# Last stage tile by tile in a written order, products of 64 rows, one pass backwards, wo's splits moved and put on GpSimd

## The chip, the cores and the metric

The kernel runs on one core of one Trainium2 chip. The metric is the device time of one execution in microseconds (us); lower is better. Matrix products run on TensorE (PE in the profile; its weight loads are PEld), element-wise work and reductions on VectorE (DVE), activations and copies on ScalarE (ACT), further element-wise work on GpSimd (POOL), and SyncE (SP) issues all DMAs of this kernel.

## What is computed

One block of a network on x, 2048 tokens of 1024 features, all in float32. Cut to what matters:

```python
xn = layernorm(x)
q, k, v = split_heads(xn @ wqkv)                  # 32 heads of 32
pq, pk = q @ w_phi, k @ w_phi                     # one 32x32 matrix for each head
phi_q = concat(softmax(pq), softmax(-pq))         # 64 features a head; phi_k likewise
kv = einsum("bhsf,bhsd->bhfd", phi_k, v)
z = sum(phi_k, over tokens)
o = (phi_q @ kv) / (phi_q @ z + 1e-6)
s = merge_heads(o) @ wo
g = silu((silu(xn @ w1) * (xn @ w3)) @ w2)        # w1, w3: 1024 x 3584; w2: 3584 x 1024
out = x + s * g
```

The quotient of a softmax needs no division of its own: with e = exp(p - max) for the first sign and the like for the second, the kernel keeps e of both signs and rho, the ratio of their two sums for each token and head, and divides once in the last stage.

## The kernel before

A large product is made with one level of a seven-product scheme (`ORDER` names the seven; "A" operands come from the activations, "B" operands from the weights), and each float32 operand is split into a high and a low float32r half (`split`: ACT copies the high half, DVE subtracts it for the low one), so that each product is three passes of matmuls of 128x512.

1. **Start.** The first half of the tokens is normalized and turned, and w_phi is folded into the weights of queries and keys.
2. **Gate and up** (`gate_up`, L595, matmuls on L622). Two halves of tokens, 28 column blocks, seven products each; a step is one product of 12 matmuls. A planner puts side work beside the steps: `at(step, f)` hangs f behind a step, `room` looks for a step with room on DVE. The side work prepares what later stages load: the second half of x, the operands of keys and values, w2's operands (`side_w`, in the second half, with blocks from two rooms of eight that go round), and the split of wo (`side_split`, 16 pieces of 128x512, in the first half; DVE subtracts, and the split is stored to `wo_d`).
3. **Three passes over 8 pairs of token tiles**: the queries (`query_heads`, L882), then two halves of keys and values (`heads`, L817). Each pair needs seven operands of 512 KB, which `reload` fetches a pair ahead. Each pass has seven weight operands of 2 MB: `fetch` loads two of them at the start of the last pair but one of the pass ahead, and five in the last pair, each behind the product that last used its place. The query pass stores e (`e_d`, L871) and rho (L906) to HBM through rooms that the next pass uses for its own features (`room_ev`, L785, filled on L830).
4. **w2** (`product`, L1106). Seven rounds over 8 pairs; `acc` in 16 slabs takes the sums. From the last round on, a slab whose pair is done goes through silu and is stored (`gate`), and is then room for the last stage: e's tiles are loaded (`load_e`) and prepared (`prep`).
5. **Last stage.** For each tile of 128 tokens, `prep` multiplies e by z on POOL (L1082, two instructions of 128x1024), sums on DVE (L1084, two), makes the factors with five short instructions, scales e (L1092, two) and transposes it in blocks of 32 (L1093, two). `attend` multiplies the transposed e by kv with 32-row, 32-column products (L1208) for a batch of two or four tiles and one half of the heads; ACT and DVE split the outcome into `oT`. `finish` makes the product with wo (`project`, L101, 24 matmuls), multiplies by the gate on DVE (L1222, `pm` from PSUM), adds x on POOL (L1223) and stores. For each half of the columns `finish` loads the gate `g` and x `xr`; SP runs in the order that is written, so those loads stand behind the store of the half before:

```python
nc.sync.dma_start(g, g_d[i][:, cs])
nc.sync.dma_start(xr, x[i * P:(i + 1) * P, cs])
```

In this stage only PE and SP run in the written order; on the other engines a scheduler sets it when the kernel is built. The batches are `[[0, 1], [2, 3], [4, 5], [6, 7], [8, 9, 10, 11], [12, 13, 14, 15]]`, and a batch is attended while the last tile of the batch ahead is finished.

## Time and profile before

| | |
|---|---|
| time, median of 3 runs | 2563.17 us (2562.22 to 2564.5) |
| the profiled execution, its own time | 2558.65 us |
| its span, first to last instruction | 2556.7 us |
| busy: PE, DVE, ACT, POOL | 94%, 70%, 34%, 9% of the span |
| mean granted TensorE clock | 0.971 |
| DMA | 586.52 MB, mean 229 GB/s |

A busy PE is not yet a PE at its peak, since its matmuls are pipelined and overlap in the records. So the rows to look for are those in which PE stood idle, with what released it, and those in which the granted clock is under 1.00. The profile speaks of `issue` where an engine waited for nothing that it shows.

### The profile page before, as it was taken

Reading aid. Unit: us, or ns where it says so; the run is one execution under the profiler, and the core shown is the slowest. Engines: PE = TensorE matmul, PEld = TensorE weight load, DVE = VectorE, ACT = ScalarE, POOL = GpSimd, SP = SyncE. Lnnn points to the kernel's source line nnn. Section 1 sums busy time; section 2 is a strip of 40 time slices with the busy share of each in tenths; the row PEclk is TensorE's granted clock in tenths of the full one; section 3 lists DMA queues with packets and bytes.
Section 4 is the critical chain, followed back from the end, with each engine's and each line's share of the span. In section 5 each row is a group of like instructions: output and inputs, shape, how many; then the busy total and the mean of one; then the engine's idle time right before and its main releaser. Section 6 shows DMA issues by size and latency. Waiting matters only on the chain.

```text
span 2556.7 us, 39191 instructions
## 1 busy us (share of the span) xinstructions
PE 2397.5 (94%) x15346; PEld 1965.3 (77%) x15346; DVE 1793.3 (70%) x2827; ACT 856.9 (34%) x1501; POOL 239.8 (9%) x206
## 2 busy tenths in 40 slices
PE   7999999999999999999969999999999999788388
PEld 6888877888888888887848878888888887566266
DVE  8777787755888888746746656657778887945641
ACT  6454555433455545432311111243222223300000
POOL 1000000000000000002310000001111112223321
PEclk9999999999999999999989999999999999988689
DMA  5346899978888887659897587344444336723333
GB/s 216 132 166 217 294 386 376 349 246 253 280 290 285 301 293 265 235 212 347 295 411 286 175 341 244 134 183 173 173 165 151 107 144 205 267 98 126 117 119 118
DMA packets 290793, 586.52 MB, mean 229 GB/s; under 512 B 23856, under 2 KB 141232, under 8 KB 287920
## 3 DMA queue, kind: packets, MB, share of 16 engines
q1 hardware_dynamic: 290608, 584.02, 64.4%
q8 instruction: 121, 1.98, 0.3%
q14 instruction: 64, 0.52, 0.1%
HBM read 378.93 MB, written 205.00 MB: 228 GB/s over the span
## 4 chain that ended last, share of the span: by engine, by line
PE 77%; DMA 9%; DVE 7%; issue 3%; POOL 2%; ACT 1%; SPq 1%; POOLq 0%; DVEq 0%; ACTq 0%
PE bankb L622 22%; PE bankb L1106 11%; PE bankc L622 11%; PE bankb L817 7%; PE banka L622 6%; PE bankc L1106 5%; PE bankc L817 3%; PE banka L1106 3%; PE bankb L882 2%; DMA acc<-e_d 2%; PE banka L817 2%; DMA xr<-in_x 1%; POOL ez L1082 1%; PE pm L101 1%; POOL g L1223 1%
## 5 line engine op out<-in xcount | busy, mean ns | idle before, releaser
L93 DVE TENSOR_TENSOR bo<-rw,bo 128x512 fp32r<-128x512 f32 x336 | 230.9, 689 | 160.2 <-ACT bo L92 158.5
L92 ACT CAST bo<-rw 128x512 fp32r<-128x512 f32 x336 | 206.5, 617 | 27.9 <-PE banka L622 5.8
L1106 PE MATMUL bankb<-bo,as 128*128 128x512 f32 x816 | 201.5, 389 | 3.5 <-DVE acc L1118 3.5
L1106 PEld LDWEIGHTS bankb<-bo,as 128*128 128x128 f32 x816 | 153.0, 188 | 36.1 <-DVE acc L1118 4.4
L622 PE MATMUL bankb<-op0S,bo 128*128 128x512 f32 x672 | 163.6, 392 | 5.0 <-ACT u L656 3.1
L622 PE MATMUL bankb<-op0A,bo 128*128 128x512 f32 x672 | 160.4, 393 | 5.1 <-DVE u L664 4.2
L622 PE MATMUL bankc<-op0S,bo 128*128 128x512 f32 x672 | 162.5, 391 | 0.3 <-DVE op0S L93 0.3
L622 PE MATMUL bankb<-op1S,bo 128*128 128x512 f32 x672 | 161.4, 389 | 0.0
L622 PE MATMUL bankc<-op1S,bo 128*128 128x512 f32 x672 | 161.2, 389 | 0.0
L622 PE MATMUL bankb<-op1A,bo 128*128 128x512 f32 x672 | 157.6, 390 | 0.0
L101 PE MATMUL pm<-wos,oT 128*128 128x512 f32 x576 | 154.2, 428 | 2.9 <-DVE g L1222 2.9
L1106 PE MATMUL bankc<-bo,as 128*128 128x512 f32 x576 | 148.3, 391 | 4.7 <-DVE as L93 4.7
L622 PEld LDWEIGHTS bankb<-op0A,bo 128*128 128x128 f32 x672 | 124.8, 188 | 33.2 <-DVE u L664 6.5
L622 PEld LDWEIGHTS bankb<-op0S,bo 128*128 128x128 f32 x672 | 124.9, 188 | 32.9 <-ACT u L656 4.3
L622 PEld LDWEIGHTS bankb<-op1A,bo 128*128 128x128 f32 x672 | 125.9, 188 | 27.4 <-DVE u L664 1.3
L622 PEld LDWEIGHTS bankb<-op1S,bo 128*128 128x128 f32 x672 | 126.0, 188 | 26.5 <-ACT u L656 0.3
L622 PEld LDWEIGHTS bankc<-op1S,bo 128*128 128x128 f32 x672 | 126.1, 188 | 26.2
L622 PEld LDWEIGHTS bankc<-op0S,bo 128*128 128x128 f32 x672 | 125.3, 188 | 26.3 <-DVE op0S L93 0.7
L101 PEld LDWEIGHTS pm<-wos,oT 128*128 128x128 f32 x576 | 119.0, 209 | 31.6 <-DVE g L1222 3.3
L862 POOL TENSOR_TENSOR eq<-q,mm 128x512 f32<-128x512 f32 x24 | 25.3, 1053 | 1220.9 <-DVE mm L860 1163.4
L1106 PEld LDWEIGHTS bankc<-bo,as 128*128 128x128 f32 x576 | 108.2, 188 | 28.9 <-DVE as L93 6.4
L1208 PE MATMUL po<-acc,kvr 32*32 32x64 f32 (+1 forms) x3072 | 46.6, 283 | 80.4 <-issue 35.0
(245 smaller groups left out, 4502.1 us busy)
## 6 DMA issues: line engine op xcount, KB each, us to landing
rw<-in_w SPq DMA_DIRECT2D x112, 512.0 KB, 5.1
hr<-h_d SPq DMA_DIRECT2D x56, 512.0 KB, 3.4
h_d<-h SPq DMA_DIRECT2D x111, 256.0 KB, 5.4
xoS<-xo_d0S SPq DMA_DIRECT2D x48, 512.0 KB, 7.9
xoS<-xo_d1S SPq DMA_DIRECT2D x48, 512.0 KB, 3.8
xoA<-xo_d0A SPq DMA_DIRECT2D x36, 512.0 KB, 7.8
xoA<-xo_d1A SPq DMA_DIRECT2D x36, 512.0 KB, 3.5
e_d<-eq SPq DMA_DIRECT2D x32, 512.0 KB, 7.6
```

The costliest lines, as they stand in the source:

```text
L92: nc.scalar.copy(hi, src)
L93: (by or nc.vector).tensor_sub(lo, src, hi.bitcast(F))
L101: nc.tensor.matmul(p, xT[dch][:, a], w(dch, b), start=n == 0, stop=n == 3 * ND - 1)
L622: nc.tensor.matmul(bank[b], bos[tb, f][bn][:, w, k], ao[an][:, u, k], start=first and n == 0, stop=LAST[b] == an and n == 11, skip_group_c ...
L817: nc.tensor.matmul(bank[b], xo[an][:, u, k], wb[bn][:, w, k], start=an in ("A11", "A12", "S1") and n == 0, stop=LAST[b] == an and n == 11, ...
L862: eng.tensor_sub(e[:, :, 0], p3, mm[:, 0, :].unsqueeze(2).to_broadcast([P, 16, DH]))
L882: nc.tensor.matmul(bank[b], xo[an][:, u, k], wb[bn][:, w, k], start=an in ("A11", "A12", "S1") and n == 0, stop=LAST[b] == an and n == 11, ...
L1082: nc.gpsimd.tensor_mul(ez[c], e_slab(t, c), zb[c])
L1106: nc.tensor.matmul(bank[b], t[:, u, pos + k], bos[kb, bn, k][:, w], start=first and n == 0, stop=LAST[b] == an and n == 5, skip_group_chec ...
L1208: nc.tensor.matmul(ev[32 * j:32 * j + 32, a, k], kvr[c][sl, j, s, k], et[sl, :, 4 * k + j, s], start=s == 0, stop=s == 1, skip_group_check ...
L1223: (nc.vector if i + 1 == NT else nc.gpsimd).tensor_add(g, g, xr)
```

## The change

- **Last stage.** All five engines run in the written order, one tile t to a step. A step makes the first half of wo's product for t, the pair sums of t+2, the small products of t+1 for one half of the heads, twelve matmuls of the second half of t, the small products for the other half of the heads, and twelve more.
- **64 rows.** e is stored with the sign outside the head (`p (s h f)`), and loaded so that a partition block of 64 holds both signs of 32 tokens. `attend` then multiplies 64 rows by 32 columns, and sums over the signs inside the product: 32 matmuls for a tile and half of the heads, where it had been 128 for two or four tiles. The denominator's sum over the signs is a product with a 0/1 matrix (`add_pairs`, a matmul of 128x64), and the factors become a reciprocal and two products with `w_all`, which holds 1 and rho.
- **Loads ahead of stores.** g and x are loaded a tile ahead and whole (512 KB each), ahead of the stores of the tile.
- **Second pass backwards.** The first pass of keys and values goes from pair 7 to pair 0, so that at both changes of pass the operands in place are used again, and a `reload` of 3.5 MB falls away. The first two weight operands of the next pass are fetched in the fourth and fifth pair, not both in the seventh.
- **wo's splits** go from the first to the second half of gate and up, every ninth step, and their subtraction from DVE to POOL. `side_w` uses three groups of five blocks.

```diff
-    def side_split(d, src, s0):
-        r = []
 
         def load():
-            r.append(flat(blk("wso")))
-            nc.sync.dma_start(r[0], src)
+            nc.sync.dma_start(blk2(15), src)
+
+        def do():
+            t = qp.tile([P, 2, 512], R, name="wso", tag="q")
+            split(t[:, 0], t[:, 1], blk2(15), nc.gpsimd)
+            at(s0 + 6, lambda: nc.sync.dma_start(d, t.bitcast(F)))
 
         at(s0, load)
-        store_quad(s0 + 4, d, lambda: r[0], "wso")
+        at(s0 + 4, do)
...
-        side_split(wo_d[c][k], wo[k * P:(k + 1) * P, c * 512:(c + 1) * 512], FIRST_STEP + 64 + 11 * m // 2)
+        side_split(wo_d[c][k], wo[k * P:(k + 1) * P, c * 512:(c + 1) * 512], HALF + 10 + 9 * m)
...
-        for i in range(len(pairs)):
-            nxt, end = {}, i + 1 == len(pairs)
+        order = range(len(pairs))[::-1] if c == 1 else range(len(pairs))
+        for pos, i in enumerate(order):
+            nxt, end = {}, pos + 1 == len(pairs)
...
-                        if i + 2 == len(pairs) and not last:
-                            for m in range(2):
-                                wbn.update(fetch(3 + c, m))
-                        if not (end and last):
-                            nxt.update(reload((i + 1) % len(pairs)))
+                        if pos in (3, 4) and not last:
+                            wbn.update(fetch(3 + c, pos - 3))
+                        if not end:
+                            nxt.update(reload(order[pos + 1]))
...
-            xo = nxt
+            xo = xo if end else nxt
...
             elif i == 4:
-                prep(0)
+                factors(0)
+                z_sums(1)
+                scale(0, 0)
+            elif i == 5:
+                add_pairs(1, "kv")
+                scale(0, 1)
                 load_e(2)
             elif i == 6:
-                prep(1)
+                factors(1)
+                scale(1, 0)
                 load_e(3)
+            elif i == 7:
+                z_products(2)
...
-    in_order(ENG.SP, ENG.PE)
+    in_order(ENG.SP, ENG.PE, ENG.DVE, ENG.Pool, ENG.Activation)
...
+            for j in range(4):
+                for a in range(2):
+                    sl = slice(64 * a, 64 * a + 64)
+                    nc.tensor.matmul(po[32 * j:32 * j + 32, a, 64 * k:64 * k + 64], kvs[sl, j, c, k], et[sl, :, 4 * k + j],
+                                     start=True, stop=True, skip_group_check=True)
...
+    for t in range(NT):
+        load_e(t + 4)
+        p = out_half(t, 0)
+        if prev:
+            gated(t - 1, 1, prev, False)
+            store_out(t - 1, 1)
+        load_g(t + 1)
+        z_sums(t + 2)
+        z_products(t + 3)
+        scale(t + 1, 1)
+        gated(t, 0, p, t + 1 == NT)
+        store_out(t, 0)
+        add_pairs(t + 2, "us")
+        lows = [attend(t + 1, 0)]
+        factors(t + 2)
+        scale(t + 2, 0)
+        prev = out_half(t, 1, lambda: lows.append(attend(t + 1, 1)))
+        for do in lows:
+            if do:
+                do()
```

Here `out_half` is wo's product for one half of the columns (24 matmuls, with `mid` called after twelve), `gated` the product with the gate and the sum with x, `z_products` the two products on POOL, `z_sums` the two sums on DVE and a product with `w_all`, `factors` the reciprocal and a product, `scale` one scaling and one transpose.

How the order changes is shown at three places. On PE at the start of the last stage, before; `po` is the outcome of the small products, `pm` that of wo's, and a row's last number counts matmuls:

```order
L1106 MATMUL bankb<-bo,as 128x512 x6
L1208 MATMUL po<-acc,kvr 32x64 x256
L101 MATMUL pm<-wos,oT 128x512 x33
L101 MATMUL pm<-late,oT 128x512 x12
L101 MATMUL pm<-wos,oT 128x512 x3
L1208 MATMUL po<-acc,kvr 32x64 x128
L101 MATMUL pm<-wos,oT 128x512 x24
```

The same place in the changed kernel, where `us` is the outcome of the pair sums:

```order
L1133 MATMUL bankb<-bo,as 128x512 x6
L1252 MATMUL po<-acc,kvs 32x64 x64
L1267 MATMUL pm<-wos,oT 128x512 x24
L1105 MATMUL us<-own 128x64
L1252 MATMUL po<-acc,kvs 32x64 x32
L1267 MATMUL pm<-wos,oT 128x512 x6
L1267 MATMUL pm<-late,oT 128x512 x6
L1252 MATMUL po<-acc,kvs 32x64 x32
```

The 256 small products that stood ahead of the first product with wo are 64, and the bursts of 128 between the tiles are two of 32 for each tile.

On DVE in the middle of the last stage, before, one tile's rows:

```order
L1084 TENSOR_REDUCE own<-ez 128x32 x2
L1222 TENSOR_TENSOR g<-pm,g 128x512
L1086 TENSOR_TENSOR own<-own 128x32
L1087 TENSOR_TENSOR own<-own 128x32
L1088 RECIPROCAL own<-own 128x32
L1089 TENSOR_TENSOR own<-own 128x32
L1092 TENSOR_TENSOR acc<-acc,own 128x1024 x2
L1093 STREAM_TRANSPOSE acc<-acc 128x1024 x2
L93 TENSOR_TENSOR oT<-po,oT 128x4x4x32 x2
```

The same engine in the changed kernel, one step:

```order
L1275 TENSOR_TENSOR g<-pm,g 128x512
L1098 TENSOR_REDUCE own<-ez 128x32 x2
L1099 TENSOR_TENSOR own<-own,rho 128x64
L1119 TENSOR_TENSOR acc<-acc,own 128x1024
L1120 STREAM_TRANSPOSE acc<-acc 128x1024
L1275 TENSOR_TENSOR g<-pm,g 128x512
L1111 RECIPROCAL own<-us 128x64
L1112 TENSOR_TENSOR own<-own,rho 128x64
L1119 TENSOR_TENSOR acc<-acc,own 128x1024
L1120 STREAM_TRANSPOSE acc<-acc 128x1024
L1258 TENSOR_TENSOR oT<-po,oT 128x2x4x64 x2
```

The work for one tile, which stood together, is cut into pieces that belong to the tiles t, t+1 and t+2, and the two rows on `oT`, for which PE's next tile waits, stand at the end of the step.

On SP where the query pass goes over into the first pass of keys and values, before; `op3` are the weights of that pass, `xo` the operands of a pair, `e_d` and `rho_d` the stores of the query pass:

```order
L871 DMA e_d_236<-eq 128x1024
L167 DMA op3T_11001<-wkv_d1T_114 128x4096
L871 DMA e_d_232<-eq 128x1024
L871 DMA e_d_236<-eq 128x1024
L906 DMA rho_d_244<-rho 128x64
L587 DMA xoA_11066<-xo_d0A_87 128x1024
L587 DMA xoA_11068<-xo_d0A_88 128x1024
L587 DMA xoS_11070<-xo_d0S_89 128x1024
```

The same place in the changed kernel:

```order
L863 DMA e_d_236<-eq 128x1024
L167 DMA op3T_10964<-wkv_d1T_114 128x4096
L863 DMA e_d_232<-eq 128x1024
L863 DMA e_d_236<-eq 128x1024
L899 DMA rho_d<-rho 128x2x32
L579 DMA xoA_11029<-xo_d1A_94 128x1024
L579 DMA xoA_11031<-xo_d1A_95 128x1024
```

The operands behind the last store are those of the second pair of the new pass (the changed kernel's first pair is pair 7, whose operands are in place); before, seven operands of the first pair had been queued ahead of these stores, and those of the second behind them.

More of the change, by code (lines that the diff above doesn't have):

```diff
@@ L542, in side_w @@
                 at(at_, then)
-        for m in slots:
-            free[m] = at_
+        free[u % 3] = at_
         assert at_ < len(events) - 3 * 7 - 4, at_
-    taken, free = [6], {m: HALF + 14 for m in range(6)}
     def side_store(m, s0):
@@ L805, in tile_kernel, with heads @@
     pkv, out_now = None, []
-    def heads(i, xo, wb, steps, pend):
+    def heads(first, last, xo, wb, steps, pend):
         nonlocal pkv
-        bank, first, last = {}, i == 0, i + 1 == len(pairs)
+        bank = {}
         for b, an, bn in ORDER:
@@ L1032, in tile_kernel @@
         load_b(0, n)
-    wos, zb, kvr, ez = {}, [], [], []
+    wos, xrs, ezs, us = {}, [], [], {}
     def load_wo(k):
@@ new lines, in add_pairs, with factors, scale @@
+    def add_pairs(t, tag):
+        if t >= NT:
+            return
+        us[t] = ps.tile([P, 512], F, name="us", tag=tag, bufs=1)[:, :64]
+        nc.tensor.matmul(us[t], own[:, :P], part_of(t, 0), start=True, stop=True)
+    def factors(t):
+        if t >= NT:
+            return
+        r, by = part_of(t, 1), part_of(t, 2)
+        nc.vector.reciprocal(r, us.pop(t))
+        nc.vector.tensor_mul(*(v.rearrange("p (c g h) -> p c g h", c=2, g=2) for v in (by, r)), w_all[:, t])
+    def scale(t, c):
+        if t >= NT:
+            return
+        e = e_slab(t)[:, c]
+        e3 = e.rearrange("p (n f) -> p n f", f=DH)
+        nc.vector.tensor_mul(e3, e3, part_of(t, 2)[:, 32 * c:32 * c + 32].unsqueeze(2).to_broadcast([P, H, DH]))
+        nc.vector.transpose(et_slab(t, c), e)
@@ L1146, in tile_kernel @@
                 if new is None:
[L1147 removed]
+                    for k in range(2 + 2 * BNAMES.index(bn), 4 + 2 * BNAMES.index(bn)):
                         load_wo(k)
@@ L1159, in tile_kernel @@
             if end:
-                for k in range(3, 9):
+                for k in range(2, 8):
                     load_wo(k)
@@ new lines, in out_half, with gated @@
+    def out_half(t, c, mid=None):
+        p = ps.tile([P, 512], F, name="pm", tag="mm", bufs=3)
+        n = 0
+        for h in range(2):
+            for k in range(4):
+                for a, b in PASSES:
+                    nc.tensor.matmul(p, oTs[t, h][:, a, k], wos[c, 4 * h + k][:, b], start=n == 0, stop=n == 3 * ND - 1)
+                    n += 1
+            if h == 0 and mid:
+                mid()
+        return p
+    def gated(t, c, p, last):
+        cs = slice(c * 512, c * 512 + 512)
+        nc.vector.tensor_mul(gs[t][:, cs], p, gs[t][:, cs])
+        (nc.vector if last else nc.gpsimd).tensor_add(gs[t][:, cs], gs[t][:, cs], xrs[t % 2][:, cs])
```

243 lines of the change are left out of this document (114 added, 129 removed).

## The prediction

> **What bounds the kernel now.** I read the waits of PE over the whole run first, because PE is busy almost everywhere and only its stops can be won back.
>
> ```profile
> PE po L1208 <- issue: 35.0, 15, 4.3
> PE po L1208 <- DVE acc L1093: 31.4, 1, 31.4
> PE bankb L817 <- ACT ev L830: 14.2, 1, 14.2
> PE po L1208 <- DVE oT L93: 13.2, 4, 6.2
> PE bankb L882 <- DMA xoA<-xo_d1A: 4.9, 1, 4.9
> PE bankc L1106 <- DVE as L93: 4.7, 4, 2.5
> PE bankb L622 <- DVE u L664: 4.2, 4, 1.4
> PE bankb L1106 <- DVE acc L1118: 3.7, 3, 2.0
> PE bankc L817 <- DMA op3T<-wkv_d1T: 3.6, 1, 3.6
> PE bankb L1106 <- DVE af L93: 3.4, 2, 2.2
> PE bankb L622 <- ACT u L656: 3.1, 3, 1.2
> PE bankb L1106 <- ACT af L92: 2.5, 1, 2.5
> PE bankb L817 <- DMA op3T<-wkv_d1T: 1.7, 1, 1.7
> ```
>
> Columns are microseconds in total, times, and the longest. Four places stand out. L1208, the small products of the last stage, waited 79.6 us (35.0 + 31.4 + 13.2). L882 and L817, where the query pass goes over into the first pass of keys, waited 24.4 us (14.2 + 4.9 + 3.6 + 1.7). L1106, w2's last round, 14.3 us. L622, gate and up, 7.3 us. I then took the windows that hold these places.
>
> ```profile
> 2139.00:2223.00 84.00, 68.81 (x280) 52.37 (x278) 74.78 (x106) 29.37 (x42) 27.99 (x14) 0.96 0.61 224
> 2223.00:2548.00 325.00, 241.39 (x3841) 194.31 (x3840) 153.93 (x199) 20.05 (x34) 94.77 (x54) 0.84 0.37 127
> 1284.00:1345.00 61.00, 36.62 (x140) 28.95 (x140) 26.30 (x45) 10.71 (x13) 7.54 (x9) 0.82 1.01 409
> 320.00:512.00 192.00, 184.66 (x852) 151.87 (x851) 152.65 (x239) 98.05 (x180) 0.00 (x0) 1.00 1.04 371
> ```
>
> After the length come busy times of PE, PEld, DVE, ACT and POOL, then granted clock, DMA share and GB/s. In the last stage (second row) no engine is full: DVE 154 of 325 us, POOL 95, DMA 37%, and PE 241 with a clock of 0.84. It is a chain of waits, not a full engine, so a better order can win much there. In the other two rows the DMA is full (1.01 and 1.04 of its share), and there only fewer or other transfers help.
>
> **The last stage, PE's side.** The timeline of PE gives the prices.
>
> ```profile
> 2223.99 2.45 PE L1208 MATMUL po<-acc,kvr 32*32 32x64 f32 x231 [0.79 <-DVE acc L1118]
> 2230.71 0.38 PE L1208 MATMUL po<-acc,kvr 32*32 32x64 f32 x25 [4.27 <-issue]
> 2261.49 7.33 PE L101 MATMUL pm<-wos,oT 128*128 128x512 f32 x24
> 2282.37 8.32 PE L101 MATMUL pm<-wos,oT 128*128 128x512 f32 x36
> 2290.53 2.88 PE L101 MATMUL pm<-late,oT 128*128 128x512 f32 x12
> 2476.89 3.02 PE L1208 MATMUL po<-acc,kvr 32*32 32x128 f32 x209
> 1385.50 0.77 PE L802 MATMUL pkv<-ev 128*32 128x34 f32 x64
> 1386.20 3.00 PE L817 MATMUL bankb<-op3T,xoS 128*128 128x512 f32 x12
> 2546.78 0.84 PE L101 MATMUL pm<-wos,oT 128*128 128x512 f32 x3
> 2553.65 0.34 SPq L1224 DMA_DIRECT2D out<-g  x1
> ```
>
> 36 matmuls of wo's product start within 8.16 us (2290.53 - 2282.37), 0.227 us each, so one tile's 48 take 10.9 us. A small product has two records (231 + 25 for the first 128). The new burst is 32 products, 64 records, of 64 columns. It no longer shares the array by sixteen but by eight, so the nearest row is that of 128 columns by sixteen: 3.02 us / 209 = 14.4 ns, 0.92 us for 64. The lower bound is 2.45 / 231 = 10.6 ns, 0.7 us; the upper bound is twice that, 1.4 us. I take 1.05 us, which leaves 0.1 for the change of shape, because 64 records of L802 between large products hold PE for 0.70 us (1386.20 - 1385.50) in all. The pair-sum matmul, which no row shows, I put at 0.3 us: no less than two small records, 0.03, no more than two slots of a large matmul, 0.45, and nearer to these because it stands alone. A step of PE is then 10.9 + 2 x 1.05 + 0.3 = 13.3 us.
>
> The `issue` stops come after 231 records of a burst (second row) and in no burst of 64 of L802. The new bursts have 64, so I let these 35 us go, and keep their return as a rival. The Trainium skill, TensorEngine Tiling (Array Packing), section Key Properties, says that a change of tiling mode drains TensorE. The change has four such changes in a step, against some two for a tile before; L802's row prices the pair at under 0.1 us, so the drain is in the 1.05.
>
> **The last stage, DVE's side.** These are the groups of the same stage (count, busy, mean ns).
>
> ```profile
> L1084 DVE TENSOR_REDUCE own<-ez 128x32 f32<-128x1024 f32 x29 | 35.2, 1215 | 76.2 <-POOL ez L1082 76.2
> L1092 DVE TENSOR_TENSOR acc<-acc,own 128x1024 f32<-128x1024 f32 x30 | 35.8, 1227 | 0.4
> L1093 DVE STREAM_TRANSPOSE acc<-acc 128x1024 f32<-128x1024 f32 x32 | 38.3, 1224 | 0.1
> L1222 DVE TENSOR_TENSOR g<-pm,g 128x512 f32<-128x512 f32 x32 | 22.0, 686 | 60.5 <-DMA xr<-in_x 44.9 <-DMA g<-g_d 8.0 <-PE pm L101 7.6
> L93 DVE TENSOR_TENSOR oT<-po,oT 128x512 fp32r<-128x512 f32 x32 | 21.8, 681 | 35.5 <-ACT oT L92 35.5
> L1088 DVE RECIPROCAL own<-own 128x32 f32<-128x32 f32 x15 | 5.2, 349 | 0.4
> L1082 POOL TENSOR_TENSOR ez<-acc,zb 128x1024 f32<-128x1024 f32 x28 | 66.0, 2377 | 93.5 <-DMA acc<-e_d 91.1 <-DVE own L1084 2.4
> L1223 POOL TENSOR_TENSOR g<-g,xr 128x512 f32<-128x512 f32 x30 | 38.5, 1284 | 150.5 <-DVE g L1222 140.6 <-DMA xr<-in_x 5.6 <-issue 4.3
> 2388.44 9.24 POOL L1082 TENSOR_TENSOR ez<-acc,zb 128x1024 f32<-128x1024 f32 x4 [4.88 <-DMA acc<-e_d]
> 2394.36 1.06 DVE L1086 TENSOR_TENSOR own<-own 128x32 f32<-128x32 f32 x1
> 2395.46 2.26 DVE L1087 TENSOR_TENSOR own<-own 128x32 f32<-128x32 f32 x1
> 2398.14 0.19 DVE L1089 TENSOR_TENSOR own<-own 128x32 f32<-128x32 f32 x1
> ```
>
> A step of DVE holds two gate products, two sums, two scalings, two transposes and two subtractions: 2 x (0.69 + 1.22 + 1.23 + 1.22 + 0.68) = 10.1 us, and a reciprocal and two short products, some 0.35 + 2 x 0.19, together 10.8; since neighbours overlap by under 0.1, about 10.1. POOL has 2 x 2.38 + 2 x 1.28 = 7.3 us. Both are under 13.3, but they are not free of each other. L1086 and L1087 read two operands from SBUF; beside POOL's products they took 1.06 and 2.26 us, ending where a POOL instruction ends (9.24 / 4 = 2.31 us apart), while L1089, clear of POOL, took 0.19. The sums, transposes and the rows that read PSUM show no such stretch.
>
> So I lay one step along time from DVE's first row. Gate product to 0.7; sums to 3.0. POOL adds from 0.7 to 2.0 and begins its first e product there, to 4.4. The short product with `w_all` waits for that, to 4.6 (wait 1.4). POOL's second e product is in line first, to 7.0, and the scaling waits for it (2.3). Scaling and transpose to 9.3, gate product to 9.9; POOL adds to 11.2, and the second short product, after the reciprocal at 10.3, waits for that (0.9). Scaling and transpose to 13.7, two subtractions to 14.9. Without waits it is 10.1, with them 14.9; PE is asked for 13.3. The step is therefore DVE's, 14.9 us, and PE stands about 1.6 us in each, most of it ahead of the subtractions of `oT`.
>
> The Trainium skill, GPSIMD Engine Reference, section Key points, says that GpSimd shares its SBUF interfaces with VectorE and contends with instructions that have two SBUF inputs. The trace agrees (2.26 against 0.19 us). Without the rule the step would be PE's 13.3 us.
>
> Thirteen steps at 14.9 are 193.7 us; two without their pair sums and e products 2 x 13.2; the last tile 10.9: 231.0. Ahead of them I put 7 us: two bursts, the copy and subtraction of `oT`, and the last evictions and silus of w2 that stand ahead on DVE and ACT (0.8 us at least by the 0.79 in the first timeline row; 10 at most). At the end come a product and a sum of 0.69 on DVE, the issue of 0.34 and the landing, from 2553.99 to the span's end, 2556.7: 4.7 us with hand-overs. Together 243 us. Before, the stage ran from the end of w2, 2223.2 (2223.99 - 0.79), to 2556.7, 333.5 us. **Gain 90.5 us**, between 64 (a step of 16.9) and 115 (a step of 13.3 and a start of 4).
>
> Loads: e comes in four parts of 32 partitions, 1 MB in all, g, x and the stores are 1.5 MB: 2.5 MB in 14.9 us is 168 GB/s, while the third window row shows 409. g and x are ordered a step ahead. I cost them at nothing; their cover is a whole step.
>
> **The change of pass.** At the end of the query pass DMA is full. Before, the last two pairs ask for two reloads of 3.5 MB, 14 MB of weights and 4 MB of e, 25 MB in some 38 us. The room of the last e is free only when its store has landed behind all that: the 14.2 us. Now 3.5 + 10 + 4 MB are left. The last pair begins its weights 2.7 us after its start, and 10 + 2 MB at 0.41 MB/us land by 32; the fifth product of the new pass, which adds to a bank that ACT must first copy into that room, is due at about 30 (19 + 4 x 2.72). With the copy and the backlog of the pair before I leave 5 us of 24.4: **gain 19**, between 13 and 24. The two weights put into the fourth and fifth pair make 7.5 MB per 19 us there, just under what DMA gives; I allow nothing for it beyond this range. The other change of pass has no stop in the list.
>
> **w2's last round.** DVE had 74.8 of 84 us. It loses one scaling with its transpose (2.4 us) and three sums that were made early for later tiles (3.7), about 6 us. Of 14.3 us of stops and the slow clock (0.96) I take **7 back**, between 0 and 14.
>
> **wo's splits.** They leave the stretch with a DMA share of 1.04: 16 x (0.25 + 0.5) MB = 12 MB less over some 220 us, 55 of 371 GB/s. I take **6 us** of the 7.3, between 0 and 7. Where they go, PE has no stop, so the stores, the ACT copies and 16 subtractions on POOL (1.28 us each by L1223) find cover; DVE's two-operand rows may wait for each, and the `q` tiles go round faster. **Cost 1.5 us**, between 0 and 8.
>
> The sum is 90.5 + 19 + 7 + 6 - 1.5 = 121 us. The profiled execution took 2558.65, 1.95 more than its span, so it would take 2437.7. The median of the runs is 4.5 higher; from it, 2563.2 - 121 = 2442.
>
> **Rivals.** (a) POOL and DVE fall so that the waits vanish or lie under PE: step 13.3, thirteen steps x 1.6 = 21 us less and a little at the start, 2419. For it: the order is free to drift. Against it: POOL has work ready at each of the three places. (b) The step is longer: `issue` stops return, since a step still asks for 356 instructions of PE in bursts, or the chain from the copy of `oT` binds: step 17, 27 us more, 2469. (c) The change of pass and gate and up keep their stops, as DMA stays full: 25 us lost, 2467.
>
> (d) Slower. PE's clock falls to half for the whole stage. Row 2261.49 shows 24 matmuls in 7.33 instead of 5.44 us after a burst with a stop, and the stage's clock is 0.84. Were it half throughout, a tile's 48 matmuls cost 21.8 us, the bursts about 3 and the pair sums 0.5: a step of 25.3, 10.4 more than forecast, and 15 steps and the last tile are 401 + 12 against 333.5; with the other gains of 30.5 the time is 2612. It turns the sign from 12 slow steps of 16 (121 / 10.4). Against it: L802's bursts between large products run at clock 1.00.
>
> ```profile
> 1408.00:1472.00 64.00, 64.00 (x645) 51.93 (x644) 38.02 (x52) 11.45 (x15) 0.79 (x6) 1.00 0.51 179
> ```
>
> Only bursts of 2 us with a stop of 2 us or more behind them lost it. The Trainium skill, TensorE: Matmul & The Clock Gate, Part 1, asks for an idle window of about 3.4 us; by that rule stops of 1.6 us leave the clock alone. The trace has it falling after a burst and a stop of 4 us together, which fits if a burst of small products counts as idle.
>
> **How the numbers follow.** Forecast 0.57, (a) 0.15, (b) 0.14, (c) 0.06, (d) 0.07; 0.01 for no change, a mild (d) that eats just the gain. Faster is 0.57 + 0.15 + 0.14 + 0.06 = 0.92. A measurement of this kernel can tell about 0.2%, 5 us, from no change. The forecast alone spans 2424 to 2462 by its terms' bounds taken in part; down to (a) with a cheap burst, 2408, and up to (b) and (c) with a bad start, 2482, leave out (d) and tails.
>
> **What would show it.** Right: bursts of 64 records near 1 us without `issue`; steps of 14.9 us with stops of PE before `pm` by `oT`; DVE rows L1099, L1112 and L1119 stretched; under 6 us of stops where pass 0 ends; granted clock near 1.00 in the last stage. Wrong: steps of 13.3 or 17; `issue` or clock 0.5 in the last stage; new waits on L614 in the second half of gate and up; waits of DVE for g or xr.

## The result, and the profile after

The changed kernel takes 2459.05 us (2455.37 to 2463.51), against 2563.84 us for the kernel before beside it: ratio 0.9592, interval 0.9574 to 0.9609. The forecast was 2442. The profiled execution took 2455.37 us with a span of 2453.6; before it was 2558.65 and 2556.7, so the two spans differ by 103.1 us where 121 were forecast.

These are the waits of PE after the change (total, times, longest; L1267 is wo's product, L1252 the small products, L1105 the pair sums, L810 the keys' product, L874 the queries', L1133 w2):

```profile
PE pm L1267 <- DVE oT L1258: 16.1, 12, 7.5
PE bankb L810 <- ACT ev L823: 15.5, 1, 15.5
...
PE bankb L1133 <- ACT af L92: 6.3, 2, 3.9
...
PE us L1105 <- DVE own L1099: 2.2, 1, 2.2
PE pm L1267 <- DMA wos<-wo_d: 1.9, 3, 1.3
PE bankb L874 <- ACT q L880: 1.7, 2, 1.2
```

The 35.0 us of `issue` and the 31.4 us on the transposes are gone. Of the waits that the prediction lists, two are larger than before: the one for ACT's copy `ev` at the change of pass, 15.5 us where it was 14.2, and w2's for ACT's half of the split (`af`), 6.3 where it was 2.5.

Where the stages begin is read from each product's rows: duration, then first and last start. First the kernel before, then the changed one.

```profile
L882 PE MATMUL bankb<-op2B,xoA x96: 389/389/667, 1143.9 to 1293.1; 128*128 128x512 f32 x96
L1106 PE MATMUL bankb<-bo,af x288: 388/389/793, 1667.8 to 2201.1; 128*128 128x512 f32 x144
```

```profile
L874 PE MATMUL bankb<-op2B,xoA x96: 387/389/628, 1141.4 to 1287.4; 128*128 128x512 f32 x96
L1133 PE MATMUL bankb<-bo,af x288: 388/389/796, 1654.7 to 2193.6; 128*128 128x512 f32 x144
```

Differences of first starts are the stages' lengths. The last stage begins at 2223.2 before, as the prediction has it, and at 2206.1 after (its first row below).

| stage | before | after | gain | forecast |
|---|---|---|---|---|
| up to the first query product | 1143.9 | 1141.4 | 2.5 | 6 - 1.5 |
| queries' and keys' passes | 523.9 | 513.3 | 10.6 | 19 |
| w2 | 555.4 | 551.4 | 4.0 | 7 |
| last stage | 333.5 | 247.5 | 86.0 | 90.5 |

One step of the last stage after the change, from the timeline of PE, DVE and POOL:

```profile
2264.51 5.30 PE L1267 MATMUL pm<-wos,oT 128*128 128x512 f32 x22 [0.80 <-DVE oT L1258]
2266.99 4.73 POOL L1090 TENSOR_TENSOR ez<-acc,zb 128x1024 f32<-128x1024 f32 x2
2267.93 1.53 DVE L1099 TENSOR_TENSOR own<-own,rho 128x64 f32<-128x64 f32 x1
2269.39 3.42 DVE L1119 TENSOR_TENSOR acc<-acc,own 128x1024 f32<-128x1024 f32 x1
2269.65 0.33 PE L1105 MATMUL us<-own 128*128 128x64 f32 x2
2269.91 0.86 PE L1252 MATMUL po<-acc,kvs 64*32 64x64 f32 x64
2279.32 5.29 PE L1267 MATMUL pm<-wos,oT 128*128 128x512 f32 x22 [0.81 <-DVE oT L1258]
```

From one large product to the same one a step later is 14.81 us (2279.32 - 2264.51). The first scaling (L1119) takes 3.42 us, where the kernel before had 1.227 on average; POOL's two e products end inside it, at 2271.72 (2266.99 + 4.73), and 1.09 us later it is done. The start of the stage, from the first small products to the second step's first large product, with the queue of SP (`SPq`) in it:

```profile
2206.12 1.71 PE L1252 MATMUL po<-acc,kvs 64*32 64x64 f32 x128
2208.53 6.01 PE L1267 MATMUL pm<-wos,oT 128*128 128x512 f32 x24 [0.70 <-ACT oT L1257]
2214.37 1.56 SPq L1032 DMA_DIRECT2D wos<-wo_d  x2
2216.80 1.62 SPq L1038 DMA_DIRECT2D g_d<-acc  x2
2219.30 0.32 SPq L1238 DMA_DIRECT2D g<-g_d  x1
2229.89 0.69 DVE L1275 TENSOR_TENSOR g<-pm,g 128x512 f32<-128x512 f32 x1 [11.78 <-DMA g<-g_d]
2234.49 7.35 PE L1267 MATMUL pm<-wos,oT 128*128 128x512 f32 x22 [7.50 <-DVE oT L1258]
```

DVE, now in written order, stands 11.78 us at the first gate product, because the load of `g` is ordered behind wo's last loads and the stores of silu. PE stands 7.5 us behind it, and its next 22 matmuls take 7.35 us, not 5.30. Counted, like the step above, from the third matmul of the first large product, which here starts at about 2208.98 (2208.53 + 2 x 0.227), the first step lasts 25.5 us, against 14.81 for a later one.

### The profile page after: what moved, and what is told of

It is laid out like the page before. It is cut to its first block, busy times and chain, and to the rows that moved or that the text cites. A ratio compares the mean times of both kernels' runs of the same rounds, so it can differ in the third digit from the quotient of the medians.

```text
span 2453.6 us, 37229 instructions
## 1 busy us (share of the span) xinstructions
PE 2373.6 (97%) x14354; PEld 1941.4 (79%) x14354; DVE 1837.6 (75%) x2795; ACT 854.8 (35%) x1501; POOL 268.5 (11%) x233
## 4 chain that ended last, share of the span: by engine, by line
PE 77%; DVE 12%; DMA 6%; issue 3%; ACT 1%; POOL 0%; SPq 0%; DVEq 0%; POOLq 0%; ACTq 0%
PE bankb L614 21%; PE bankb L1133 11%; PE bankc L614 10%; PE bankb L810 7%; PE bankc L1133 6%; PE banka L614 5%; PE bankc L810 3%; PE bankb L874 3%; PE banka L1133 3%; DVE acc L1119 2%; PE banka L810 2%; PE bankc L874 1%; PE pm L1267 1%; DVE own L1098 1%; DVE bo L93 1%
## 5 line engine op out<-in xcount | busy, mean ns | idle before, releaser
L1133 PE MATMUL bankb<-bo,as 128*128 128x512 f32 x816 | 200.9, 389 | 0.0
L1133 PEld LDWEIGHTS bankb<-bo,as 128*128 128x128 f32 x816 | 153.2, 188 | 31.8
L1267 PE MATMUL pm<-wos,oT 128*128 128x512 f32 x576 | 145.3, 402 | 18.7 <-DVE oT L1258 16.1
L1133 PE MATMUL bankc<-bo,as 128*128 128x512 f32 x576 | 150.2, 396 | 0.8 <-ACT as L92 0.7
L1267 PEld LDWEIGHTS pm<-wos,oT 128*128 128x128 f32 x576 | 107.1, 191 | 48.8 <-DVE oT L1258 21.8
L1133 PEld LDWEIGHTS bankc<-bo,as 128*128 128x128 f32 x576 | 109.6, 191 | 25.4 <-ACT as L92 2.0
L93 POOL TENSOR_TENSOR wso<-room,wso 128x512 fp32r<-128x512 f32 x16 | 24.2, 1512 | 961.4 <-ACT wso L92 845.0
L1145 DVE TENSOR_TENSOR acc<-bankb,acc 128x512 f32<-128x512 f32 x152 | 104.1, 686 | 27.0 <-PE bankb L1133 19.8
```

The source lines that it names most:

```text
L93: (by or nc.vector).tensor_sub(lo, src, hi.bitcast(F))
L1133: nc.tensor.matmul(bank[b], t[:, u, pos + k], bos[kb, bn, k][:, w], start=first and n == 0, stop=LAST[b] == an and n == 5, skip_group_chec ...
L1145: nc.vector.tensor_add(c, pb, c)
L1267: nc.tensor.matmul(p, oTs[t, h][:, a, k], wos[c, 4 * h + k][:, b], start=n == 0, stop=n == 3 * ND - 1)
```

## Experiments

All times are medians. The interval of a ratio is about 0.0017 to either side, 4 us, so smaller differences are read from the traces. A ratio is against the kernel before, run beside it; between two kernels of the table the interval is wider, some 6 us by an estimate from the two.

| kernel | us | ratio | interval |
|---|---|---|---|
| changed kernel | 2459.05 | 0.9592 | 0.9574 to 0.9609 |
| passes forward | 2468.12 | 0.9618 | 0.9602 to 0.9634 |
| splits back in the first half | 2461.08 | 0.9594 | 0.9580 to 0.9608 |
| splits on DVE | 2454.88 | 0.9570 | 0.9555 to 0.9584 |
| e stored by ACT | 2453.03 | 0.9566 | 0.9549 to 0.9583 |
| no e products | 2440.31 | 0.9519 | 0.9505 to 0.9533 |
| sums later | 2443.88 | 0.9535 | 0.9519 to 0.9550 |
| g early | 2450.41 | 0.9559 | 0.9545 to 0.9574 |
| e stored by ACT, late weights | 2453.51 | 0.9572 | 0.9558 to 0.9586 |
| third room | 2457.92 | 0.9584 | 0.9562 to 0.9606 |
| before, batches of two | 2555.77 | 0.9972 | 0.9960 to 0.9985 |
| five edits | 2419.46 | 0.9439 | 0.9420 to 0.9457 |
| six edits | 2420.36 | 0.9440 | 0.9426 to 0.9453 |

### Does POOL set the step?

**No e products.** From the first step on, POOL's two products of e with z are left out.

```diff
         z_sums(t + 2)
-        z_products(t + 3)
         scale(t + 1, 1)
```

> The changed kernel, but from the first step of the last stage on GpSimd's two products of e with z are left out (so the denominators of tiles 3 to 15 are wrong), and nothing else. Theory (DVE's short products and scalings wait for GpSimd's e products on the shared SBUF interface, and so DVE sets the step of 14.8 us): the stretched rows L1119 go back from 3.4 to 1.23 us and L1099 from 1.5 to 0.2, the step falls to PE's own 13.2 to 13.4 us, PE's stops before pm and po go under 0.3 us a step, and 12 to 13 steps x 1.5 = 18 to 20 us go: 2436 to 2441. Rival (the hand-over from PE to DVE and back over the copy of oT sets the step, GpSimd only fills slack): the rows get shorter but PE still stops for oT by over 0.8 us a step and the gain is under 6 us, 2453 to 2459.

**Sums later.** All the work, in another order: `z_sums` is cut into its sums (`z_reduce`) and its short product (`z_scale`).

```diff
+    z_reduce(2)
+    z_products(3)
...
-        z_sums(t + 2)
-        z_products(t + 3)
+        z_scale(t + 2)
         scale(t + 1, 1)
...
-        scale(t + 2, 0)
+        scale(t + 2, 0, lambda: (z_reduce(t + 3), z_products(t + 4)))
```

The function given to `scale` runs between its product and its transpose.

> The changed kernel with all its work, in another written order on DVE and GpSimd: the sums of the denominators of tile t+3 and GpSimd's e products of t+4 come after the second scaling of the step, ahead of its transpose, so that the e products run beside a transpose, a subtraction and a gate product, none of which reads two operands from SBUF, and the short products and the two scalings find GpSimd idle. Theory (waits of DVE for GpSimd set the step): laid out by hand, the step falls from 14.8 to about PE's 13.2 to 13.6 us, so 12 to 20 us go: 2439 to 2447; DVE's L1119 scaling back at about 1.23 us. Rival (the number of DVE's own operations, 10.1 us, with the hand-overs to PE and ACT in the written order, or GpSimd's own chain, sets the step): under 6 us, 2453 to 2459, or slower since a later sum delays the pair-sum product of PE.

The same 160 us of the last stage of the changed kernel, without e products, and with later sums (busy PE, PEld, DVE, ACT, POOL; clock, DMA share, GB/s):

```profile
2254.00:2414.00 160.00, 145.89 (x1949) 113.66 (x1948) 158.15 (x142) 12.95 (x22) 77.53 (x44) 1.00 0.58 168
```

```profile
2254.00:2414.00 160.00, 160.00 (x2148) 129.55 (x2148) 137.71 (x159) 14.12 (x24) 33.21 (x25) 1.00 0.62 180
```

```profile
2254.00:2414.00 160.00, 159.88 (x2148) 129.16 (x2147) 153.90 (x159) 14.11 (x24) 83.05 (x47) 1.00 0.65 185
```

DVE was the full engine: 158.15 of 160 us, with 142 operations. Without e products it does 159 in 137.71 us, PE is full, and the step, from the same product of PE twice, is 13.12 us (2317.38 - 2304.26). With later sums it is the same, read from two pair sums (2325.77 - 2312.65):

```profile
2312.65 0.33 PE L1116 MATMUL us<-own 128*128 128x64 f32 x2
2325.77 0.33 PE L1116 MATMUL us<-own 128*128 128x64 f32 x2
```

Without e products the time falls by 0.0073 of the kernel before, 19 us (0.9592 - 0.9519). With later sums the 83.05 us of POOL's work are all there, PE is as full, and the time still falls by 0.0057, 15 us. The 4 us between the two are within the intervals; part of them is in the start, where the stop for `oT` is 10.6 us with later sums and 8.2 without e products. Theory shown: DVE's wait for POOL set the step, and the written order placed it there.

### The start of the last stage

**g early.** The first `load_g` is written ahead of wo's last eight loads, in w2's last round.

```diff
                 if new is None:
+                    if an == "S1":
+                        load_g(0)
...
-    load_g(0)
     for c in range(2):
         attend
```

> The changed kernel, but the loads of g and x for the first tile of the last stage are written ahead of the last eight loads of wo in the last round of w2, where they stood behind them and behind stores of g. Theory (the stop of 7.5 us at the start of the last stage is DVE waiting for g, which stands in SP's row): the wait of DVE for g goes, the stop shrinks to 1 to 3 us, and the kernel gains 4 to 7 us: 2452 to 2455. Rival (DMA is full there, so what is taken from g is put on wo's loads or e's): the stop stays over 5 us or moves to PE waiting for wos, gain under 2 us: 2457 to 2460.

```profile
PE pm L1271 <- DVE oT L1262: 8.7, 11, 0.9
```

The stop of 7.5 us has gone: the longest is 0.9. The wait for wo's loads rose by 1.0 us (1.9 to 2.9). By the ratios it gains 0.0033, 8 us, and in the trace the last stage is 7.5 us shorter (from 2206.86 to 2446.8). That is the stop itself; whether the slow matmuls behind it (7.35 - 5.30 = 2.05) came on top can't be told from this, since a stop of 2.4 us for wo's loads, with slow matmuls behind it, took the place of one of 1.3.

### The change of pass

**Passes forward.** All passes go from pair 0 to 7, reload at the change, and fetch two weights in the seventh pair, as before.

```diff
-        order = range(len(pairs))[::-1] if c == 1 else range(len(pairs))
+        order = range(len(pairs))
...
-            xo = xo if end else nxt
+            xo = nxt
```

> The changed kernel with its three passes all forward, both reloads at the changes of pass back, and the first two weights fetched together in the seventh pair, as before. Reading of the trace: the change took the stops at the end of the query pass from 24.4 to about 18 us, so undoing it costs 6 to 8 us, some 2466 us, and the stop on ACT ev is near 14 us again. The forecast's price of the turn was 19 us: if that was right and something else ate it, the time is near 2478 us.

```profile
PE bankb L810 <- ACT ev L823: 13.2, 1, 13.2
PE bankb L874 <- DMA xoA<-xo_d1A: 5.3, 1, 5.3
PE bankc L810 <- DMA op3T<-wkv_d1T: 3.9, 1, 3.9
PE bankb L810 <- DMA op3T<-wkv_d1T: 2.1, 1, 2.1
```

24.5 us of stops, as before the change (24.4); the changed kernel has 17.9 there (15.5 + 1.7, and 0.7 for an operand's reload). Turning back and fetching the two weights earlier are together worth those 6.6 us, and 0.0026 or 7 us by the ratios; no run parts the two. What holds the rest is in the timeline of the changed kernel: the start of the last query pair, SP's queue, the copy, and PE behind it.

```profile
1279.60 12.33 SPq L863 DMA_DIRECT2D e_d<-eq  x4
1284.92 2.88 PE L874 MATMUL bankb<-op2B,xoA 128*128 128x512 f32 x12
1295.14 0.42 SPq L167 DMA_DIRECT2D op3T<-wkv_d1T  x1
1307.65 3.32 SPq L863 DMA_DIRECT2D e_d<-eq  x2
1329.91 0.59 ACT L823 COPY ev<-bankb 128x512 f32<-128x512 f32 x1 [19.28 <-DMA rho_d<-rho]
1330.55 4.82 PE L810 MATMUL bankb<-op3T,xoS 128*128 128x512 f32 x12 [15.55 <-ACT ev L823]
```

SP stands at the stores of the pair ahead, whose e has not been made yet by ACT, so the first weight is ordered at 1295.14, 10.2 us after the pair's start. The copy waits for the pair's third store, issued at 1307.65; the trace's answer on that one store gives its time to landing:

```profile
DMA to landing us min/median/max: 22.2/22.2/22.2
```

That is 1329.85, just ahead of the copy. The releaser that the row names, `rho_d`, was ordered at 1313.28 and took 17.6 us, to 1330.9, so it can't have been what the copy waited for.

**e stored by ACT.**

```diff
-        nc.sync.dma_start(e_d[pairs[i][j]][:, c], ef)
+        nc.scalar.dma_start(e_d[pairs[i][j]][:, c], ef)
...
-                nc.sync.dma_start(rho_d.rearrange(
+                nc.scalar.dma_start(rho_d.rearrange(
```

> The changed kernel with the stores of e and rho in the query pass issued by ACT, not by SP. Theory: the weights of the next pass start late because SP, which works in order, stands at the stores of the pair before, and the last e then lands behind 12 MB; with the stores on another engine's queue the weights start within 3 us of their place and the store no longer stands behind them, so the stop of 15.5 us falls under 4 and the time to about 2446 us. Rival: the volume binds, 14 MB at 0.41 MB/us take 34 us in any order; then the stop stays above 10 us, on the weights if not on ACT ev, and the time is 2455 to 2460 us.

```profile
1288.95 5.76 SPq L167 DMA_DIRECT2D op3T<-wkv_d1T  x3
1325.34 5.49 PE L810 MATMUL bankb<-op3T,xoS 128*128 128x512 f32 x12 [9.22 <-ACT ev L823]
```

The weights start 6 us earlier, 2.9 us after the pair's start (1286.04, seven products of 2.72 us ahead of the pass's end at 1305.08), and the stop falls to 9.2 us. That lies between the two expectations: SP's hold was a part, and the rest needed another cause. The third store now lands 15.9 us after its order, at 1324.68. From the first weight's order to there the DMA is full, and it moved 14.42 MB where the prediction had 10 + 2:

```profile
1288.95:1324.68 35.73, 27.17 (x120) 22.15 (x118) 21.09 (x38) 8.42 (x10) 6.23 (x6) 0.94 1.00 404
DMA packets 2054, 14.42 MB, mean 404 GB/s; under 512 B 466, under 2 KB 466, under 8 KB 1412
```

**Late weights.** On top of that edit, the last two weights two products later.

```diff
-    NEXT = ({0: 2, 1: 3, 2: 4, 3: 5, 4: 6},
+    NEXT = ({0: 2, 1: 3, 2: 4, 5: 5, 6: 6},
```

> The changed kernel with e's and rho's stores issued by ACT (the run before of that kind took 2453.0 and left a stop of 9.2 us on the copy that waits for e's last store) and with the last two of the five weight operands that the last query pair fetches ordered two products (5.4 us) later, so that the third e store of the pair has some 2 to 4 MB less ahead of it. Theory (the store lands late because of the volume ordered ahead of it): the stop of ACT's copy shrinks from 9.2 to 0 to 5 us, nothing waits for the two weights, and 4 to 8 us go: 2445 to 2449. Rival (the weights, not the store, are the true limit, since DMA is full up to the fifth product of the new pass): the stop moves to PE waiting for op3 operands, about the same sum: 2452 to 2456.

It did not test its theory: the stop stayed at 9.5 us, because the orders hardly moved. The fifth weight was ordered 16.67 us after the first with the old table (1305.62 - 1288.95) and 17.20 with the new (1303.70 - 1286.50), rows of `op3T` in SP's timeline. SP's own waits in this stretch name what held them, with the old table and then with the new:

```profile
SPq L167 <- DMA op3T<-wkv_d1T: 10.5, 2, 5.7
SPq L167 <- DMA op3T<-wkv_d1T: 11.0, 2, 5.7
```

The fourth and the fifth order waited until the first and the second weight had landed: the first, ordered at 1288.95, took 10.5 us, to 1299.45, and the fourth went out at 1299.51. So the pace of the landings set these orders, not the table.

**Third room.** The first features and values of the keys go into two `q` tiles.

```diff
     def room_ev():
+        if firsts:
+            e, v = firsts
...
+        if c == 0:
+            firsts += [quad("ev", F), quad("ev", F)]
```

> The changed kernel, but the first features and values of the keys' pass go into two free rooms of the q pool (free because the pass turns back and loads no operands for the next pair) instead of the room of the last query pair's e; nothing else. Theory (the 15.5 us stop at the change of pass is the wait of one ACT copy for the store of e out of that room, which lands late behind 12 MB): the copy no longer waits, the next one that needs the old room comes three products (8 us) later and finds it free or nearly so, the stop of ACT ev goes to 0 to 5 us, and with the slow clock behind it 11 to 17 us go: 2442 to 2448. Rival (DMA volume is the limit itself, whatever waits for it, since 12 MB have to land in some 30 us): PE stops about as long for operands of the new pass (op3 weights) or for the next copy, gain under 6 us, 2453 to 2459.

```profile
PE bankc L817 <- ACT ev L838: 15.0, 1, 15.0
```

The rival held. The stop went to the next copy, which needs the old room one product later, not three, and it is as long: the third store, ordered at 1311.12, took 21.6 us, to 1332.7, and the copy began at 1332.82. One more room doesn't help while that store lands so late.

### wo's splits

**Back in the first half** (on DVE, from `store_quad`):

```diff
-        side_split(wo_d[c][k], wo[...], HALF + 10 + 9 * m)
+        side_split(wo_d[c][k], wo[...], FIRST_STEP + 64 + 11 * m // 2)
```

> The changed kernel with wo's splits back in the first half of gate and up, their subtraction on DVE. Reading of the trace: the first half gets its 7.3 us of stops back and the second half loses 4.7 us, so 2 to 3 us more, some 2462 us. The forecast had 4.5 us. If the second half's stops have nothing to do with the splits (side_w's groups of five, say), they stay and the cost is 7 us.

**In the second half, on DVE:**

```diff
-            split(t[:, 0], t[:, 1], blk2(15), nc.gpsimd)
+            split(t[:, 0], t[:, 1], blk2(15))
```

> The changed kernel with wo's splits where they are now, but subtracted on DVE and not on POOL. If POOL's subtractions cost by holding DVE's two-operand instructions back, the 4.7 us of stops in the second half of gate and up fall to 1 or 2, some 2456 us. If the extra transfers and q tiles cost, the stops stay at 4 to 5 us or grow by DVE's 16 x 0.6 us of work, 2459 to 2462 us.

Windows of the two halves. PE is busy for all 334.00 us of the first in the changed kernel and with splits on DVE, so the rows are the second half of the changed kernel, both halves with splits back, and the second with splits on DVE:

```profile
530.00:1140.00 610.00, 605.19 (x2659) 497.18 (x2658) 469.83 (x711) 281.39 (x519) 24.20 (x16) 1.00 0.81 279
```

```profile
196.00:530.00 334.00, 326.67 (x1522) 270.37 (x1521) 260.90 (x413) 171.04 (x313) 0.00 (x0) 1.00 0.94 325
530.00:1140.00 610.00, 609.52 (x2689) 503.61 (x2688) 461.09 (x718) 275.41 (x507) 0.00 (x0) 1.00 0.77 261
```

```profile
530.00:1140.00 610.00, 607.52 (x2672) 500.01 (x2672) 465.90 (x729) 282.88 (x520) 0.00 (x0) 1.00 0.81 281
```

PE's idle time is the length less its first number. The move takes 7.3 us out of the first half (334.00 - 326.67) and brings the second to 4.8 (610.00 - 605.19), where 0.5 stand with the splits back (610.00 - 609.52) and 2.5 with DVE in POOL's place (610.00 - 607.52). So the rival, that the second half's stops come from `side_w`'s groups of five, accounts for 0.5 us at most. In time the move can't be told from nothing (0.9594 against 0.9592). The kernels with splits on POOL and on DVE differ by 0.0022, with intervals that overlap; the traces say 2.3 us (607.52 - 605.19).

### Short bursts in the kernel before

```diff
-    batches = [..., [6, 7], [8, 9, 10, 11], [12, 13, 14, 15]]
+    batches = [..., [6, 7], [8, 9], [10, 11], [12, 13], [14, 15]]
```

> The kernel before, with the batches of four tiles in its last stage cut into batches of two, so that a burst has 128 small products at the most, not 256; nothing else. It tells how much of the last stage's gain of some 86 us short bursts alone can bring, without the written order, the 64 rows and the early loads. Theory (the issue stops come with long bursts, and the stops on the transposes with the pile of preparations before a batch of four): 35.2 us of issue stops fall to under 12 and the stops on transposes of 31.4 us to under 20, 20 to 35 us go: 2529 to 2544. Rival (the stops come from loads behind stores and the order of DVE, and only move): 0 to 10 us, 2553 to 2565.

```profile
PE po L1208 <- issue: 57.6, 19, 5.0
```

```profile
2332.28 2.60 PE L1208 MATMUL po<-acc,kvr 32*32 32x64 f32 x243
2337.88 0.46 PE L1208 MATMUL po<-acc,kvr 32*32 32x64 f32 x13 [3.00 <-issue]
```

The rival held. The 31.4 us on the transposes went, but `issue` rose from 35.0 to 57.6 us, and just 7 us were gained (0.9972), a twelfth of what the last stage gained. A burst of 256 records still stops, here after 243, in other bursts of this run after 103 to 239. In the kernel before, too, stops came after fewer records than the 231 that the prediction reads: one after 95, at 2236.04. Neither the changed kernel's bursts of 64, nor its one of 128 at 2206.12, stops. Whether that comes from their length or from their shape (64 rows, not 32) no run tells.

### All that paid, together

**Five edits:** sums later, g early, e stored by ACT, splits on DVE, third room.

> The changed kernel with five edits together: sums later in the step, g and x of the first tile ahead of wo's last loads, stores of e and rho issued by ACT, wo's splits subtracted on DVE, and two rooms of the q pool for the first features of the keys' pass. Each but the last was run alone and took 15.2, 8.6, 6.0 and 4.2 us off the changed kernel's 2459. If they add, and the fifth brings what is left of the stop at the change of pass (9 us and some slow clock): 2414 to 2422. If those at the start of the last stage and at the change of pass overlap more (stops that move to the next load): 2422 to 2432.

2419.46 us: 0.0153 of the kernel before, 39 us, below the changed kernel. One by one the ratios make 0.0146, so within the intervals the edits add up. The largest stop that stands is the one on the copy `ev`.

**Six edits:** also the last two rho stores behind the weights, on SP. Its reason came from the run with e stored by ACT: packets, MB and share of the two queues (q1 is SP's, q10 ACT's) from 1305 to 1310.

```profile
q1 hardware_dynamic: 143, 2.08, 97.2%
q10 hardware_dynamic: 139, 0.07, 4.7%
```

```diff
+                if i < 6:
+                    nc.scalar.dma_start(dst, src)
+                else:
+                    late_rho.append((dst, src))
...
+            for dst, src in late_rho:
+                nc.sync.dma_start(dst, src)
```

> The kernel of five edits (2419.5 us, of which 8.6 us are a stop on a copy that waits for the third store of e of the last query pair), with one edit more: the rho stores of the last two query pairs are ordered by SP behind the weights, not by ACT between the stores of e. Theory: while weights and e's stores are under way on two queues, the DMA engines take a packet of each in turn, whatever its size (143 to 139 packets in 1305 to 1310 of the run with e on ACT, but 2.08 to 0.07 MB), so the 256 packets of a rho store, 32 KB in all, hold e's stores up by 256 packets of 16 KB, some 9 to 10 us; without them the third store lands before its room is needed: the stop of 8.6 us goes to 0 to 1.5 us, with the slow clock behind it 9 to 11 us, 2408 to 2411. Rival (volume alone: the store cannot land before the 10 MB of weights, or SP's or another wait takes over, such as PE for a weight that comes later): the stop stays over 5 us or moves, 2415 to 2421.

```profile
q1 hardware_dynamic: 114, 1.61, 75.0%
q10 hardware_dynamic: 118, 0.42, 20.6%
```

The rows are those of the two queues with the sixth edit, from 1300 to 1305. The rival held on the time (2420.36, the stop on the copy `ev` 8.7 us). The turns are as the theory says (114 packets to 118), but e's own packets are small too. By an estimate from these rows, 0.42 MB in 5 us is 1.6 MB in a pair's 19 us, and a pair stores 2.1 MB, so e falls behind by itself. By answers on single stores, the last pair's second store now landed after 15.5 us instead of 19.0, but its third, for which the copy waits, after 16.2 against 16.1.

## Why the prediction was right, and where not

**The last stage: right.** 86.0 us for 90.5; step 14.81 for 14.9; burst 0.86 for 1.05; pair sum 0.33 for 0.3; no `issue`; clock 1.00 from 2254 to 2414 (0.97 over the whole stage, with its slow first step). The rows named in advance are stretched, and by what was laid out: L1099 took 1.53 us and 0.23 clear of POOL (1.3 for 1.4), L1119 3.42 and 1.23 (2.2 for 2.3), L1112 1.00 and 0.23 (0.8 for 0.9). L1099 and L1119 are short again without e products. Rival (a) priced correctly what an order without those waits is worth: a step of 13.12 us for its 13.3, and it needs no less work, only later sums. How the 86 us divide among the written order, the 64 rows and the early loads no run tells. The Trainium skill, SBUF — State Buffer, section Who interferes with whom, says that a DVE instruction with two SBUF inputs contends with a GpSimd instruction that reads SBUF; this agrees with 3.42 against 1.23 us, with and without e products beside it.

**The first step: mis-sized, since "their cover is a whole step" failed.** It is true of every tile but the first, whose g had no step ahead of it. That step took 25.5 us where 14.9 were forecast, with PE's stop of 7.5 us in it, against 0.8 in a later step. The 7 us ahead of it were 2.41 (2208.53 - 2206.12). These two errors partly cancel, by luck, and so the stage missed by 4.5 us and not by over 10.

**The change of pass: the mechanism was right, the size was off by half.** 19 us were forecast; stops fell by 6.5 and the passes by 10.6, under the least of the range, 13. The step that failed is "the last pair begins its weights 2.7 us after its start": it was 10.2, because SP stands at e's stores first. I had not counted what stands on SP ahead of the loads that are moved. The step behind it, that 5 us would be left, rested on that. But e stored by ACT, which starts the weights 2.9 us after the pair's start, leaves 9.2 us, so it was not the whole error. "10 + 2 MB at 0.41 MB/us land by 32" failed too: with the weights on time, the rate was as forecast (404 GB/s), but 14.4 MB moved, and the store landed 38.6 us after the pair's start (1324.68 - 1286.04). What can't be parted is volume and turns: the store goes beside weights that come in packets four times its size (1.61 MB / 114 = 14.1 KB, 0.42 / 118 = 3.6), and no run has less volume ahead of it or larger packets of e.

**wo's splits: the gain of 6 was right (7.3), the cost of 1.5 too low (4.8),** inside its bounds of 0 to 8. POOL's turn with DVE is 2.3 of it, 0.5 stands without the splits too, and the other 2.0 are not settled.

**w2's last round: near.** DVE's busy time in it fell, from 74.78 us in the last 84 to 65.73, and the stops from 15.1 us in all to 9.2 (6.3 + 2.2 + 0.7). But the largest now waits for ACT, and with one of 3.9 us in it the clock over those 84 us is 0.92, not 0.96; the stage is shorter by 4.0, of 7 forecast. No run tested this term.

Of the other rivals, (b) and (d) did not come, with no `issue` and a clock of 1.00 in the steps; of (c) about half did, at the change of pass.

By the table 4.5, 8.4, 2.0 and 3.0 us were missed at these four: 17.9, all of 121 - 103.1.

## What to carry to other kernels

When every engine runs in written order, lay each step along time with the waits between DVE and GpSimd in it, and put GpSimd's products beside DVE operations that read one operand from SBUF: here the same work took 13.1 instead of 14.8 us a step. Cost the first step by itself: what covers a load in the steady state is not there yet. When loads are to start earlier, look at what is written ahead of them on the queue that issues them, and at the stores that somebody waits for.

## What was not expected of the hardware

**Two DMA queues share by packets, not by bytes.** With weights on SP's queue and e and rho on ACT's, both had as many packets (143 and 139; 114 and 118), but 2.08 to 0.07 MB and 1.61 to 0.42 MB. So small packets beside large ones are slow. With five edits the first store of e behind a rho store of 32 KB landed after 24.6 us. The Trainium skill, DMA: Bandwidth & Descriptors, section Queues, rings and completion order, says that each DMA engine goes round the queues packet by packet. These counts agree.

**A long stop of PE costs more than its length.** After 15.5 and 9.2 us, the next 12 matmuls took 4.82 and 5.49 us instead of 2.88; after 7.5 us, 22 took 7.35 instead of 5.30. After 0.8 us there was no such loss (5.30, 5.29). So about 2 us or more go with each long stop, which the forecast allowed for in w2's round alone. It needs no burst ahead: after the stop of 3.1 us for `xoA` at the start of the queries, with large products alone before it, the next 12 took 5.46 us and the granted clock was 0.50. The prediction had it fall only behind bursts; and this stop is shorter than the idle window that the prediction cites.
